# A tuned attention-and-MLP kernel: the opening by pairs of heads, FP32 dummies, a later v tail, six feature tiles begun early, w_out used by quarters

## The chip, the cores and the metric

The kernel runs on one core of a Trainium2 chip. The core has five engines that each work through their own list of instructions in order: TensorE (PE, matmuls; weight loads are shown as PEld), VectorE (DVE), ScalarE (ACT), GpSimd (POOL) and SyncE (SP). PE writes to PSUM only; DVE and ACT read it from there. SP and POOL issue the DMA transfers between HBM and SBUF. The metric is device time of one launch in microseconds, lower is better: 337.65 us as the median of 3 runs (337.59 to 338.38) for the kernel before.

## What is computed

Attention with a forget gate over 8 batches, 8 heads, 576 positions and a head size of 64, then an MLP with a tanh GELU over all 4608 tokens, model size 512, feature size 2048.

```python
scores = (1 / sqrt(D)) * q @ k.T
cum = cumsum(log(clip(f, 1e-4, 1.0)))            # along the positions
scores = where(causal, -1e9, scores + cum[:, None] - cum[None, :])
attn = softmax(scores)
x = (attn @ v).transpose(0, 2, 1, 3).reshape(B * S, H * D)
h = x @ w_in
g = 0.5 * h * (1 + tanh(c * (h + 0.044715 * h**3)))
out = g @ w_out
```

The decay splits into a factor for the query, which the softmax cancels, and a factor for the key. The kernel holds the latter in `wT` and multiplies v by it (`vw`); the same factors make the denominators.

## The kernel before

Four heads of a batch are a quad; there are 16, two for each batch. For a quad, q and k are loaded with a cast to bf16 (`load_qk`, POOL's queue) into one of two buffers and turned by DVE (`transpose_qk`). `score_round` computes transposed scores in three rounds r = 0, 1, 2 into two PSUM tiles of two banks, one for each pair of heads (`bank_pair`), and ACT takes the exp of each pair's tile into `pt`. Then come denominators (`denominators`, `reciprocals`) and two output products (`attn_out`, `normalise`) into `xT`. `make_vw` forms `vw` of a quad on POOL or DVE.

The MLP runs in chunks of 512 tokens. `mlp_in(j)` makes 16 feature tiles, two to a PSUM pair, with four matmuls each (dt = 0 to 3), and `gelu` writes `gT`. `mlp_out(j)` is a generator: each pull is one feature tile's matmul into an output tile of 128 tokens (16 pulls to a tile, 64 to a chunk), or four matmuls of 32 columns each where other tiled matmuls stand around it. The output tile lies in the PSUM pool "m", which has two buffers; after the sixteenth pull DVE copies it to `o_st` and SP stores it. `step(i, j, fill, fills)` weaves the three score rounds of quad i, the products of quad j and `fills[r]` pulls of the generator.

Everything is recorded under a manual schedule: an engine executes its instructions in the order in which the code records them.

What the change touches:

- `startup` (lines 379 to 455): the loads, the gate's cumulative sums, dummy matmuls on `blank` (`warm_up`), then quads 0 and 1 in "early" rounds without the last 64 queries (`early_rounds`), with the causal mask added on PE by a matmul of the identity with `lows` (line 200), `late_scores` for the last 64 queries, and the first chunk of the MLP. PSUM tags "s" (two pairs), "x" (one pair) and "p" (two banks) are shared out there. In before, four feature tiles are begun with dt = 0, 1 while DVE normalises quad 1.
- The loads on POOL's queue in the order of line 414 on: v of batch 0 (heads 4 to 7), four parts of w_in, q and k of quad 2, four quarters of w_out, q and k of quad 3, v of batch 1 (heads 0 to 3). Heads 0 to 3 of batch 0's v, and heads 4 to 7 of batch 1's, come over SP's queue.
- `mlp_out` (lines 347 to 366), and the pulls of batch 0 (lines 517 to 523): 6, then 10, 8, 8 in `step(2, ...)`, 4, 6, 5 in `step(3, ...)`, 6, 6, 5 in `step(4, ...)`.
- In `step`, `make_vw(2)` is recorded on DVE in round 2 (line 480), ahead of that round's pulls (line 481).

Of the kernel before, what the change touches and what calls it, by code (L numbers as in the profile page):

```python
# [8 lines left out]
FP32 = mybir.dt.float32  # L9
# [7 lines left out]
def kernel(  # L17
# [80 lines left out]
    blank = singles.tile([128, 512], BF16, name="blank")  # L98
# [18 lines left out]
    def load_v(b, eng=nc.sync, heads=slice(0, H)):  # L117
        return [eng.dma_start(
            out=v_nat[b % 2][r:, t, heads, :],
            in_=v[b, heads, s0:s0 + 128 - r, :].rearrange("h p d -> p h d"),  # L120
        ) for t, r, s0 in [(t, 0, 128 * t) for t in range(TAIL)] + [(TAIL, 128 - LAST, S - LAST)]]
# [48 lines left out]
    def scores(i, tiles, cols, k0, q0, nq, c0, m0=0, m=128, fresh=False):  # L170
        for c in cols:
            for h in range(4):
# [8 lines left out]
    def score_round(i, r, tags=("s", "s"), early=False):  # L181
        off, parts = (early_rounds if early else rounds)[r]
        n = sum(x[2] for x in parts)
        tiles = [bank_pair(x, "ps_s") for x in tags]
        if r == 0:
            for c in range(2):
                scores(i, tiles, (c,), 0, 0, 512, 0, 0, 64, True)
                scores(i, tiles, (c,), 64, 64, 448, 64, 64, 64, True)
                scores(i, tiles, (c,), S - LAST, S - LAST, LAST, 0, 64, 64)
        else:  # L190
            c0 = 0
            for (t, q0, nq) in parts:
                scores(i, tiles, range(2), 128 * t, q0, nq, c0, fresh=(c0 == 0))
                c0 += nq
        if early:
            for g in range(2):
                c0 = 0
                for (t, q0, nq) in parts:
                    for x in range(2):
                        nc.tensor.matmul(tiles[g][:, x, c0:c0 + 128], ident, lows[t > 0],  # L200
                                         start=False, stop=True, skip_group_check=True)
                    c0 += nq
        for g in range(2):
            nc.scalar.activation(pt[i % 2][:, 2 * g:2 * g + 2, off:off + n],  # L204
                                 tiles[g][:, :, 0:n], AF.Exp, scale=scale)
# [141 lines left out]
    def mlp_out(j):  # L347
# [5 lines left out]
        for n, c0, c1 in parts:  # L353
            ps = pools["m"].tile([128, D_MODEL], FP32, name="pso", tag="m")
            c = 128 * (n % 8)
            for ft in range(N_FT):
                w = out_cols[0]
                for m in range(0, 128, w):
                    nc.tensor.matmul(ps[m:m + w, c0:c1], gT[:, ft, c + m:c + m + w],  # L359
                                     w_out_sb[:, ft, c0:c1], start=(ft == 0),  # L360
                                     stop=(ft == N_FT - 1), skip_group_check=True)
                if ft == N_FT - 1:
                    st = ostage_pool.tile([128, D_MODEL], FP32, name="o_st", tag="o")
                    nc.vector.tensor_copy(st[:, c0:c1], ps[:, c0:c1])  # L364
                    nc.sync.dma_start(out=out[128 * n:128 * n + 128, c0:c1], in_=st[:, c0:c1])
                yield
# [12 lines left out]
    def startup():  # L379
# [8 lines left out]
        warm = pools["p"].tile([128, 512], FP32, name="warm", tag="p")  # L388
        warm_up(warm, 11)
# [17 lines left out]
        warm_up(warm, 6)  # L407
# [4 lines left out]
        after(load_v(0, heads=slice(0, 4))[0], q0)  # L412
        make_vw(0, nc.vector, 0, TAIL)
        after(load_v(0, nc.gpsimd, slice(4, 8))[0], k1)
# [18 lines left out]
        score_round(1, 1, ("x", "s"), True)  # L433
# [3 lines left out]
        make_vw(1, nc.vector, 0, TAIL)  # L437
        score_round(1, 2, ("s", "x"), True)
        late_scores()
        reciprocals(1, early_product(1, den_groups(1), single("po")))  # L440
        po = bank_pair("x", "po")
        nums = [early_product(1, out_groups(1, y), po[:, y, :]) for y in range(2)]
# [9 lines left out]
        for u in range(2):  # L452
            gelu(0, u, phs[u])
        for u in range(2, N_FT // 2):
            mlp_in(0, (u,), "x" if u % 3 == 2 else "s")
# [41 lines left out]
    with tc.manual_schedule():  # L497
# [6 lines left out]
        for b in range(B):  # L504
# [61 lines left out]
```

## Time and profile before

| | |
|---|---|
| median of 3 runs | 337.65 us (337.59 to 338.38) |
| the profiled execution | 338.67 us |
| its span, first to last instruction | 337.0 us |
| read from HBM, written | 36.85 MB, 9.44 MB |
| issues of v on POOL's queue (128 KB), median to landing | 8, 6.8 us |
| issues of w_in parts (512 KB), median to landing | 4, 11.0 us |
| issues of w_out quarters (512 KB), median to landing | 4, 17.8 us |

The profile is one execution on the chip. A row of the timeline gives the start in us from the first instruction, the length of a merged group of instructions, engine, source line, operation, tiles written and read, shape and count; in brackets stands the idle time of the engine before the group and what ended it. The chain of work that ended last is followed back from the end, at each step to what released an instruction. The table of stages gives the busy time of each engine in a stretch, the granted PE clock as a share, the busy share of the DMA engines and the bytes moved.

### The profile page before, as it was taken

To read this page: it belongs to the slowest core of one execution; us is meant where nothing else is said; L and a number is where in the kernel's file an instruction comes from. 1 tells how busy PE (TensorE), PEld (TensorE's weight loads), DVE (VectorE), ACT (ScalarE), POOL (GpSimd) and SP (SyncE) were. 2 spreads that over 40 slices of the span, in tenths; PEclk is the share of its full clock that TensorE was granted. 3 is DMA by queue.
4 is the path that set the end of the run, shared out by engine and by line. 5 is a ranking of instruction groups with operands and counts; after the bars stand their busy time and mean duration, and the time that the engine had idled before them with its cause. 6 is when DMAs were issued, how large, how long until landed. Compare 5 with 4: busy or idle time off the path is not lost.

```text
span 337.0 us, 10056 instructions
## 1 busy us (share of the span) xinstructions
PE 327.8 (97%) x4549; PEld 160.8 (48%) x4571; DVE 124.8 (37%) x174; ACT 191.3 (57%) x206; POOL 115.1 (34%) x159
## 2 busy tenths in 40 slices
PE   7979999999999999999999999999999999999996
PEld 2544534444444444444478444444444454444444
DVE  7682176622526144604442342524330450000121
ACT  4875777767565757467555756576647704553000
POOL 6833258924534145242725162405520300000000
PEclk9999999999999999999999999999999999999999
DMA  7999999696117801491029310921000110000112
GB/s 133 204 180 211 216 216 207 143 210 131 64 35 153 161 35 64 98 205 45 33 71 205 74 65 33 186 57 66 36 31 0 35 64 33 0 0 28 67 69 87
DMA packets 45578, 33.29 MB, mean 99 GB/s; under 512 B 34304, under 2 KB 34560, under 8 KB 45536
## 3 DMA queue, kind: packets, MB, share of 16 engines
q0 software_dynamic: 7232, 14.81, 24.3%
q1 hardware_dynamic: 38304, 17.85, 19.7%
q8 instruction: 35, 0.57, 0.7%
q14 instruction: 7, 0.06, 0.1%
HBM read 36.85 MB, written 9.44 MB: 137 GB/s over the span
## 4 chain that ended last, share of the span: by engine, by line
PE 93%; issue 2%; DVE 1%; ACT 1%; DMA 1%; POOL 0%; POOLq 0%
PE ps_h L323 37%; PE pso L359 36%; PE po L250 10%; PE ps_s L173 9%; ACT pt L204 1%; DMA f_sb<-in_f_dram 1%; PE ps_s L200 1%; PE warm L377 1%; DVE cum_sb L400 0%; POOL pt L229 0%; DVE kT L142 0%; DVE qT L142 0%; ACT f_sb L399 0%; POOLq L561 0%; DVE f_sb L398 0%
## 5 line engine op out<-in xcount | busy, mean ns | idle before, releaser
L359 PE MATMUL pso<-w_out_sb,gT 128*32 128x512 bf16 (+2 forms) x1669 | 133.4, 377 | 0.5 <-issue 0.3
L323 PE MATMUL ps_h<-xT,w_in_sb 128*128 128x512 bf16 (+1 forms) x625 | 125.9, 357 | 2.4 <-issue 1.7
L332 ACT ACTIVATE gT<-ps_h 128x1024 bf16<-128x1024 f32 (+1 forms) x81 | 74.1, 928 | 70.9 <-PE ps_h L323 70.9
L204 ACT ACTIVATE pt<-ps_s 128x1024 bf16<-128x1024 f32 (+1 forms) x96 | 91.1, 1002 | 40.9 <-PE ps_s L173 38.3
L323 PEld LDWEIGHTS <-w_in_sb 128*128 128x128 bf16 x640 | 61.9, 98 | 65.3 <-issue 5.2
L359 PEld LDWEIGHTS <-gT 128*32 128x32 bf16 (+1 forms) x1675 | 59.8, 97 | 55.0 <-issue 1.0
L229 POOL TENSOR_SCALAR_AFFINE_SELECT pt<-pt 128x512 bf16<-128x512 bf16 (+1 forms) x70 | 44.1, 638 | 101.0 <-ACT pt L204 99.9
L364 DVE COPY o_st<-pso 128x512 f32<-128x512 f32 (+1 forms) x37 | 24.9, 674 | 87.6 <-PE pso L359 87.6
L281 DVE STREAM_TRANSPOSE den<-po 128x576 f32<-128x576 f32 (+2 forms) x17 | 12.7, 748 | 70.0 <-PE po L250 70.0
L154 POOL TENSOR_TENSOR vw<-v_nat,wT 128x1280 bf16<-128x1280 f32 (+1 forms) x26 | 37.7, 1471 | 0.9 <-DVE rec L283 0.7
L291 DVE TENSOR_TENSOR xT<-po,rb 128x576 bf16<-128x576 f32 (+1 forms) x32 | 23.8, 748 | 34.9 <-PE po L250 34.8
L173 PE MATMUL ps_s<-qT,kT 32*128 32x64 bf16 (+8 forms) x944 | 33.4, 286 | 1.0 <-ACT pt L204 0.6
L250 PE MATMUL po<-pt,vw 128*32 128x64 bf16 (+6 forms) x768 | 27.5, 277 | 0.0
L173 PEld LDWEIGHTS <-kT 32*128 32x128 bf16 (+1 forms) x944 | 14.6, 97 | 24.3 <-issue 20.9
L142 DVE STREAM_TRANSPOSE kT<-k_c 128x576 f32<-128x576 f32 x16 | 19.9, 1245 | 10.0 <-DMA k_c<-in_k_dram 10.0
L142 DVE STREAM_TRANSPOSE qT<-q_c 128x576 f32<-128x576 f32 x16 | 19.9, 1242 | 1.4 <-DMA q_c<-in_q_dram 1.3
L250 PEld LDWEIGHTS <-vw 128*32 128x32 bf16 x832 | 13.6, 96 | 13.8 <-issue 7.1
L112 POOL DMA_DIRECT2D k_c<-in_k_dram x16 | 9.1, 570 | 30.0 <-DVE kT L142 24.7
L250 PE MATMUL po<-pt,w_bf 128*32 128x64 bf16 (+8 forms) x384 | 14.3, 276 | 0.1
L285 DVE STREAM_TRANSPOSE rb<-rec 128x576 f32<-128x576 f32 (+2 forms) x17 | 12.6, 743 | 0.6
L112 POOL DMA_DIRECT2D q_c<-in_q_dram x16 | 8.6, 535 | 8.5 <-DVE qT L142 5.7
L332 ACT ACT_TABLE_LOAD x8 | 10.3, 1283 | 0.1
(43 smaller groups left out, 72.4 us busy)
## 6 DMA issues: line engine op xcount, KB each, us to landing
out_dram<-o_st SPq DMA_DIRECT2D x35, 256.0 KB, 2.0
v_nat<-in_v_dram SPq DMA_DIRECT2D x24, 256.0 KB, 5.9
k_c<-in_k_dram POOLq DMA_DIRECT2D x16, 288.0 KB, 6.3
q_c<-in_q_dram POOLq DMA_DIRECT2D x16, 288.0 KB, 7.2
w_in_sb<-in_moe_w_in_dram POOLq DMA_DIRECT2D x4, 512.0 KB, 11.0
w_out_sb<-in_moe_w_out_dram POOLq DMA_DIRECT2D x4, 512.0 KB, 17.8
v_nat<-in_v_dram SPq DMA_DIRECT2D x14, 128.0 KB, 5.1
v_nat<-in_v_dram POOLq DMA_DIRECT2D x8, 128.0 KB, 6.8
```

What stands on the lines that cost most here:

```text
L112: return [nc.gpsimd.dma_start(out=dst[i % 2].rearrange("p a d -> p (a d)"), in_=src[b, h0:h0 + 4].rearrange("h (p a) d -> (h p) (a d)", p=32))
L142: nc.vector.transpose(out=dst[i % 2].rearrange("p s c -> p (s c)").bitcast(FP32) .rearrange("p (t a) -> p a t", a=S // 32), in_=src[i % 2] ...
L154: eng.tensor_mul(vw[i % 2][:p, slot:slot + z - a], v_nat[(i // QPB) % 2][:p, a:z, h0:h0 + 4, :], wT[:p, i, a:z, :].unsqueeze(3).to_broadca ...
L173: nc.tensor.matmul(tiles[h // 2][m0:m0 + m, h % 2, c0:c0 + nq], kT[i % 2][32 * h:32 * h + 32, k0:k0 + m, c], qT[i % 2][32 * h:32 * h + 32, ...
L204: nc.scalar.activation(pt[i % 2][:, 2 * g:2 * g + 2, off:off + n], tiles[g][:, :, 0:n], AF.Exp, scale=scale)
L229: nc.gpsimd.affine_select(out=p[p0:p1, :, o:o + 128], in_=p[p0:p1, :, o:o + 128], compare_op=ALU.is_ge, fill=0.0, base=0, pattern=[[0, 4]] ...
L250: nc.tensor.matmul(ps[r0:r0 + w.shape[-1], o:o + nq], w, rhs[:, h, col:col + nq], start=(n in fresh), stop=(n in (0, len(parts) - 1)), ski ...
L291: nc.vector.tensor_mul(xT[:, 2 * (i % QPB) + y, t0:t0 + n], po, rbs[i][:, 0:n])
L323: nc.tensor.matmul(ph[:, o:o + m], w[:, dt], xT[:, dt, a:a + m], start=(dt == 0 and o == 0), stop=(dt == N_DT - 1), skip_group_check=True)
L332: nc.scalar.activation(gT[:, 2 * u + y:2 * u + y + n, o:o + CHUNK], ph[:, y:y + n, :], AF.Gelu_apprx_tanh)
L359: nc.tensor.matmul(ps[m:m + w, c0:c1], gT[:, ft, c + m:c + m + w], w_out_sb[:, ft, c0:c1], start=(ft == 0), stop=(ft == N_FT - 1), skip_gr ...
L364: nc.vector.tensor_copy(st[:, c0:c1], ps[:, c0:c1])
```

## The change

Masks of the first round are added to PSUM ahead of its scores (`first_round`); all early rounds but the first are done for one pair of heads at a time (`early_pair`), with tags s, x in turn; dummies take FP32 operands of 256 columns and fall from 11, 6, 4, 4, 2 to 5, 3, 1; the tail of v of batch 0 is loaded by one transfer for all eight heads behind w_in; quarter 0 of w_out comes ahead of q and k of quad 2; `make_vw(1)` is split in two halves; six feature tiles instead of four are begun with dt = 0, 1; `mlp_out(0)` takes tiles 0 and 1 in turns of four features; and the pulls of batch 0 are shared out anew. Its core:

```diff
-    blank = singles.tile([128, 512], BF16, name="blank")
+    blank = singles.tile([128, 256], FP32, name="blank")
...
+    v_tiles = [(t, 0, 128 * t) for t in range(TAIL)] + [(TAIL, 128 - LAST, S - LAST)]
+
+    def load_v(b, eng=nc.sync, heads=slice(0, H), tiles=slice(0, NT)):
...
+    def add_lows(r, tile, fresh=False):
+        c0 = 0
+        for (t, q0, nq) in early_rounds[r][1]:
+            for x in range(2):
+                nc.tensor.matmul(tile[:, x, c0:c0 + 128], ident, lows[t > 0],
+                                 start=fresh, stop=True, skip_group_check=True)
+            c0 += nq
...
+    def early_pair(i, r, g, tag):
+        tiles = {g: bank_pair(tag, "ps_s")}
+        part_scores(i, r, tiles, (2 * g, 2 * g + 1), early_rounds)
+        add_lows(r, tiles[g])
+        exps(i, r, g, tiles[g], early_rounds)
+
+    def first_round():
+        tiles = [bank_pair("s", "ps_s") for _ in range(2)]
+        for g in range(2):
+            add_lows(0, tiles[g], True)
+        yield
+        part_scores(0, 0, tiles, range(4), early_rounds, True)
+        for g in range(2):
+            exps(0, 0, g, tiles[g], early_rounds)
+        yield
...
-        for n, c0, c1 in parts:
-            ps = pools["m"].tile([128, D_MODEL], FP32, name="pso", tag="m")
+
+        order = [(x, ft) for x in range(len(parts)) for ft in range(N_FT)]
+        if j == 0:
+            order[:2 * N_FT] = [(x, ft) for f0 in range(0, N_FT, N_FT // 4) for x in range(2)
+                                for ft in range(f0, f0 + N_FT // 4)]
+        pss = {}
+        for x, ft in order:
+            n, c0, c1 = parts[x]
+            if ft == 0:
+                pss[x] = pools["m"].tile([128, D_MODEL], FP32, name="pso", tag="m")
+            ps = pss[x]
...
-        warm_up(warm, 11)
+        warm_up(warm, 5)
...
-        warm_up(warm, 6)
+        first = first_round()
+        next(first)
+        warm_up(warm, 3)
...
         for c in range(2):
             for u in range(QPB):
                 load_w_in(c, u)
+        load_v(0, nc.gpsimd, tiles=slice(TAIL, NT))
+        load_w_out(0)
         load_qk(2)
-        for c in range(4):
+        for c in range(1, 4):
             load_w_out(c)
...
+        make_vw(1, nc.vector, 0, 2)
...
-        for r, tags, n in ((0, ("s", "s"), 4), (1, ("x", "s"), 4), (2, ("s", "x"), 2)):
-            score_round(0, r, tags, True)
-            warm_up(warm, n)
-        score_round(1, 0, ("s", "s"), True)
+        next(first)
+        early_pair(0, 1, 0, "x")
+        early_pair(0, 1, 1, "s")
+        early_pair(0, 2, 0, "s")
+        warm_up(warm, 1)
+        early_pair(0, 2, 1, "x")
+        early_pair(1, 0, 0, "s")
+        early_pair(1, 0, 1, "s")
+        early_pair(1, 1, 0, "x")
...
-        phs = [bank_pair("s", "ps_h") for _ in range(2)]
-        for dts in ((0, 1), (2,), (3,)):
-            for ft in range(4):
-                mlp_mm(0, ft, phs[ft // 2][:, ft % 2, :], dts)
-            if dts[0] == 0:
-                for y in range(2):
-                    normalise(1, y, nums[y])
+        phs = [bank_pair(tag, "ps_h") for tag in ("x", "s", "s")]
+        for ft in range(6):
+            mlp_mm(0, ft, phs[ft // 2][:, ft % 2, :], (0, 1))
+        for y in range(2):
+            normalise(1, y, nums[y])
+        for u in range(3):
+            for y in range(2):
+                mlp_mm(0, 2 * u + y, phs[u][:, y, :], (2, 3))
+            gelu(0, u, phs[u])
...
-                pull(fill, 6, 32)
+                pull(fill, 8, 32)
                 late_outputs(bank_pair("po", "po")[:, 0, :])
-                step(2, None, fill, (10, 8, 8))
-                step(3, 2, fill, (4, 6, 5))
-                step(4, 3, fill, (6, 6, 5))
+                step(2, None, fill, (8, 10, 10))
+                step(3, 2, fill, (4, 5, 5))
+                step(4, 3, fill, (5, 5, 4))
```

More of the change, by code (lines that the diff above doesn't have):

```diff
@@ L179, in scores, with exps, part_scores @@
                 )
-    def score_round(i, r, tags=("s", "s"), early=False):
-        off, parts = (early_rounds if early else rounds)[r]
+    def exps(i, r, g, tile, rounds=rounds):
+        off, parts = rounds[r]
         n = sum(x[2] for x in parts)
-        tiles = [bank_pair(x, "ps_s") for x in tags]
+        nc.scalar.activation(pt[i % 2][:, 2 * g:2 * g + 2, off:off + n], tile[:, :, 0:n], AF.Exp,
+                             scale=scale)
+    def part_scores(i, r, tiles, heads, rounds=rounds, ahead=False):
@@ L191, in score_round @@
             c0 = 0
-            for (t, q0, nq) in parts:
-                scores(i, tiles, range(2), 128 * t, q0, nq, c0, fresh=(c0 == 0))
+            for (t, q0, nq) in rounds[r][1]:
+                scores(i, tiles, range(2), 128 * t, q0, nq, c0, fresh=(c0 == 0), heads=heads)
                 c0 += nq
[L195 to L202, printed above, removed]
```

63 lines of the change are left out of this document (31 added, 32 removed).

## The prediction

> **What bounds the kernel now.** First the page's first and fourth part. TensorE (PE) is at work nearly throughout, and the chain that ended last runs over it, so a change counts by how much idle time it takes from PE or gives to it.
>
> ```profile
> span 337.0 us, 10056 instructions
> PE 327.8 (97%) x4549; PEld 160.8 (48%) x4571; DVE 124.8 (37%) x174; ACT 191.3 (57%) x206; POOL 115.1 (34%) x159
> PE 93%; issue 2%; DVE 1%; ACT 1%; DMA 1%; POOL 0%; POOLq 0%
> ```
>
> The change touches the opening and batch 0 alone, so I next read the chain of the first 45 us. What the change can reach in the opening are the masks (L200) on the chain, the dummies (L377) that the chain waits behind, and a hole of 1.54 us ahead of the third matmul round of the MLP, for which the profile names no cause.
>
> ```profile
> 9.04 0.33 PE ps_s L200 x4
> ...
> 9.42 0.81 PE warm L377 x3
> ...
> 11.55 0.86 PE warm L377 x4
> ...
> 13.17 0.43 PE warm L377 x2
> ...
> 23.50 1.54 issue
> 25.04 9.67 PE ps_h L323 x44
> ```
>
> Third, busy time by stage, for the DMA. The columns after the stretch are its length, the five engines' busy time, the granted clock, the busy share of the DMA engines and GB/s.
>
> ```profile
> 15.00:20.00 5.00, 4.50 (x156) 2.82 (x148) 3.96 (x6) 4.72 (x6) 3.27 (x6) 1.00 0.97 142
> 20.00:25.00 5.00, 3.44 (x82) 1.78 (x69) 4.11 (x9) 3.22 (x3) 1.41 (x2) 1.00 1.11 206
> ...
> 35.00:40.00 5.00, 5.00 (x164) 2.88 (x170) 0.87 (x4) 3.56 (x6) 1.52 (x3) 1.00 1.12 211
> 40.00:45.00 5.00, 4.84 (x57) 1.91 (x42) 2.53 (x4) 3.63 (x5) 1.95 (x5) 1.00 1.08 238
> 45.00:50.00 5.00, 4.83 (x84) 2.25 (x88) 3.61 (x5) 3.46 (x5) 2.50 (x4) 1.00 1.00 197
> ```
>
> The DMA engines are full until about 50 us, with loads alone. So what is loaded late lands when the sum of the bytes ahead of it has been moved, however early it was asked for, and a faster opening does not hasten it. The question for this change is therefore which of those landings PE meets when it comes earlier. Fourth, the timeline around 46 us:
>
> ```profile
> 46.24 1.67 PE L359 MATMUL pso<-w_out_sb,gT 128*128 128x512 bf16 x7 [0.16 <-issue]
> 46.46 1.82 DVE L154 TENSOR_TENSOR vw<-v_nat,wT 128x1280 bf16<-128x1280 f32 x2 [0.54 <-DMA v_nat<-in_v_dram]
> 47.84 0.91 PE L173 MATMUL ps_s<-qT,kT 32*64 32x512 bf16 x24
> 48.21 0.68 DVE L364 COPY o_st<-pso 128x512 f32<-128x512 f32 x1
> ```
>
> VectorE (DVE) waits 0.54 us for v of batch 1, heads 0 to 3, starts the multiplication of quad 2 (`make_vw(2)`) at 46.46, and only then copies out an output tile, at 48.21. Before, nobody minds: it is tile 1, and PE goes on into tile 2 at once, because tile 0 had been copied long ago and the pool "m" has two buffers.
>
> **The change part by part.** *Opening* (masks in front, pairs, dummies, the early half of `make_vw(1)`, six feature tiles). On ACT the exps of both quads stand nearly back to back, with a hole here and there, so pairs can save about the mask's 0.33 us and the holes' 0.47 and 0.29:
>
> ```profile
> 14.76 5.14 ACT L204 ACTIVATE pt<-ps_s 128x1024 bf16<-128x1024 f32 x6 [0.47 <-PE ps_s L200]
> 20.19 1.94 ACT L216 ACTIVATE pt_late<-ps_s 128x1024 bf16<-128x1024 f32 x2 [0.29 <-PE ps_s L173]
> ```
>
> That is 1.1 us; the dummies removed (0.81 + 0.86 + 0.43 = 2.10) stand beside these exps and give nothing of their own. Six tiles begin with 12 matmuls in place of 8 ahead of the late normalising, four more of 0.215 (below), 0.86 us of useful work into the hole of 1.54. Together 2.0 us; the bounds are 0 and 2.10 + 1.54 + 0.33 = 4.0. The FP32 dummies have no row. The nearest are the FP32 transposes of 64 columns beside the bf16 dummies:
>
> ```profile
> 1.26 4.31 PE L377 MATMUL warm<-blank 128*128 128x512 bf16 x11 [1.26 <-DVE blank L387]
> ...
> 6.21 0.49 PE L404 MATMUL small<-ident_f,cum_sb 64*128 64x64 f32 x5 [0.64 <-DVE cum_sb L400]
> 6.63 0.98 PEld L377 LDWEIGHTS <-blank 128*128 128x128 bf16 x6
> 6.63 1.47 PE L377 MATMUL warm<-blank 128*128 128x512 bf16 x6
> ```
>
> 0.49 / 5 is 0.1 us for 64 columns, so 0.4 for 256; at the slow pace of the first eleven (0.39 against 0.245 each) 0.6. Five then take 2.0 to 3.0 us and three 1.2, no more than the 4.31 and 1.47 they replace. I cost them at 0; were they twice as long, the scores would start about 2 us later, and the opening would lose its gain.
>
> *v tail behind w_in*: two transfers of 64 KB become one of 128 KB on the POOL queue. 128 KB at 206 GB/s is 0.6 us by which all four parts of w_in land sooner. It is used by `make_vw` of the tail, hidden under the features that follow. *w_out quarter 0 ahead of k and q of quad 2*: their order only; from w_out's second quarter on, the sequence of loads, with k and q of quad 3 and v of batch 1 behind it, has the same bytes ahead of it as before. So v of batch 1 still lands for a start of DVE at 46.46.
>
> *w_out by quarters*, and with it the step on which the time hangs. In `mlp_out(0)` tiles 0 and 1 now take turns, four features at a time, so tile 0 ends with the 28th matmul group and tile 1 with the 32nd, where tile 0 ended with the 16th. The fills of step 2 sum to 8 + 8 + 10 + 10 = 36 up to its end, where they were 6 + 10 + 8 + 8 = 32. So groups 33 to 36, the first of tile 2, stand on PE ahead of the scores of quad 3, and tile 2 needs the buffer of tile 0. Tile 0 can only be copied out in the last round of step 2, and there `step` records `make_vw(2)` on DVE ahead of the fills: both copies now queue on DVE behind a multiplication that waits for v. PE waits for the first copy; behind PE's wait stand the scores of quad 3 and all else on PE, and the exps of ACT.
>
> The sum. The copy ends at 48.21 + 0.68 = 48.89, the handover takes 0.04:
>
> ```profile
> 50.83 0.04 issue
> ```
>
> so PE goes on at 48.93. Before, PE had done the same work, 32 groups and the scores of step 2, by 47.84 at the latest. With the opening's 2.0 us it is there at 45.9 and stands idle for 3.0 us; with any gain from 0 to 4.0 it is there between 43.9 and 47.9, always ahead of 48.93. The opening's gain therefore falls out of the sum: the hold has to be paid from 47.84. The four groups come first, (1.67 - 0.38) / 6 = 0.215 each by the row of seven above (0.38 is the duration of one), 0.86 together; the scores of quad 3 start at 49.79, that is 1.95 later than before. They then find their buffers free, so the exps follow sooner:
>
> ```profile
> 39.79 0.66 PE L173 MATMUL ps_s<-qT,kT 32*64 32x512 bf16 x24
> ...
> 40.60 1.94 ACT L204 ACTIVATE pt<-ps_s 128x1024 bf16<-128x1024 f32 x2 [0.45 <-PE ps_s L173]
> ...
> 48.88 1.94 ACT L204 ACTIVATE pt<-ps_s 128x1024 bf16<-128x1024 f32 x2 [0.83 <-PE ps_s L173]
> ...
> 50.87 0.63 PE L173 MATMUL ps_s<-qT,kT 32*128 32x64 bf16 x14 [0.20 <-ACT pt L204]
> ...
> 51.58 1.94 ACT L204 ACTIVATE pt<-ps_s 128x1024 bf16<-128x1024 f32 x2 [0.76 <-PE ps_s L173]
> ...
> 54.26 1.94 ACT L204 ACTIVATE pt<-ps_s 128x1024 bf16<-128x1024 f32 x2 [0.74 <-PE ps_s L173]
> ...
> 57.62 1.47 PE L359 MATMUL pso<-w_out_sb,gT 128*32 128x512 bf16 x24
> ...
> 59.76 1.94 ACT L204 ACTIVATE pt<-ps_s 128x1024 bf16<-128x1024 f32 x2 [0.77 <-PE ps_s L173]
> ```
>
> 40.60 - 39.79 = 0.81 after the scores, so at 50.60 where it was 48.88: 1.72 late. Do the four groups done early come back in steps 3 and 4, whose fills fall from 32 to 28? A group there is 1.47 / 6 = 0.245 us, so 0.98 if PE sets the pace. But the exps follow each other at 2.70, 2.68 and so on up to 59.76, and the scores of a round wait for the exps of the one before (the 0.20 at 50.87): 0.74 from scores to exps and 1.94 of exps are 2.68. ACT and PE in turn set that pace, and shorter fills do not shorten it. Only the last round, which no exps follow, gets its one group back: 1.72 - 0.245 = 1.47, say 1.5. Behind it PE is dense, and I see nothing that would win it back.
>
> If PE sets the pace after all it is 1.95 - 0.98 = 0.97; if the fills give nothing back, 1.95. The profiled execution took 338.67, of which 337.0 are span and 1.7 lie around it; it would be 340.2. It stands 1.0 above the median of the runs, 337.65; from there it is **339.1**, 338.6 to 339.6 by these two bounds. What I can't price is the transfer of v: if the 128 KB of the tail now cost their 0.6 us twice, it lands that much later; if the stretch from 15 to 20 us, in which only 142 GB/s were moved, ran at 206, (206 - 142) x 5 / 206 = 1.6 us sooner. With these the range is 337.0 to 340.2.
>
> **The rivals.** *The DMA gains, and the hold shrinks to nothing:* v lands 1.6 us sooner, the copy ends at 47.3, and PE is about even: 339.1 - 1.6 = 337.5. For it speaks that the slow stretch is just where the order of loads changes; against it that the queue still issues as many transfers there.
>
> *The gain holds:* the opening's 2.0 us stay. That needs tile 0's copy by 45.9, v landed 3.0 us sooner: 337.65 - 2.0 = 335.7. The full DMA rows from 20 us on speak against it.
>
> *The clock drops in the idle time:* PE stands still for 3.0 us. [...] Against it: the granted clock is 1.00 in every row, the hole of 1.54 included; for it, that no hole of this size is in the trace. [...]
>
> *The change doesn't speed the opening:* two heads at a time fill half of the row groups, and PE could be late for the exps. Up to about 1 us of net loss it changes nothing, since the hold covers it (47.84 + 1.1 = 48.93); with 2 us lost 339.1 + 1.0 = 340.1.
>
> **How the numbers follow.** A measurement of this kernel tells about 0.3% from no change, 1.0 us. The forecast 0.58, of which some 0.06 end below 338.6 and so within it; the DMA gains 0.18; the gain holds 0.10; the clock 0.09; a slower opening 0.05. Faster: 0.10 and 0.02 of the DMA's case, 0.12. Same: 0.16 of the DMA's case and 0.06 of the forecast's, 0.22. Slower: the rest, 0.66. The range from 336.8 to 340.9 leaves out the gain that holds and the far end of the clock's case.
>
> **What would show it.** Right: a hole of about 3 us on PE ahead of the ninth group of the last round of step 2, ended by the copy of `o_st`, which ends near 48.9; the exps of quad 3 about 1.7 us later than 48.88; the hole of 1.54 us gone and the matmuls behind it, now from 25.04, about 2 us earlier. Wrong: the multiplication of quad 2 starting well before 46; or PE coming to that group after 48.9, so that the opening counts; or exps of quad 3 and 4 following each other in less than 2.6 us.

## The result, and the profile after

The changed kernel takes 341.72 us (median of four runs, 340.55 to 342.08) against 337.85 us (337.59 to 338.38) for the kernel before: 1.0107 times as long, with an interval from 1.0079 to 1.0134. It is slower, as forecast, but by 3.9 us where 339.1 meant some 1.5, and the time lies outside the range of 336.8 to 340.9. The profiled execution took 340.55 us, close to the 340.2 worked out for it.

The page of the changed kernel: PE has about 1 us more of work, and the span is 1.8 us longer than in the profiled execution before.

```profile
span 338.8 us, 10026 instructions
PE 328.9 (97%) x4535; PEld 163.6 (48%) x4556; DVE 125.3 (37%) x175; ACT 191.2 (56%) x206; POOL 115.6 (34%) x159
PE 82%; DMA 11%; issue 2%; POOL 2%; DVE 1%; ACT 1%; POOLq 0%; DVEq 0%
PE pso L394 33%; PE ps_h L350 33%; PE po L277 9%; PE ps_s L175 7%; DMA w_out_sb<-in_moe_w_out_dram 5%; DMA w_in_sb<-in_moe_w_in_dram 3%; DMA v_nat<-in_v_dram 2%; DMA k_c<-in_k_dram 2%; POOL v_nat L120 1%; DVE vw L156 1%; ACT pt L186 1%; POOL pt L256 0%; DVE o_st L399 0%; POOL w_in_sb L133 0%; POOLq L607 0%
```

In the chain of waits, DMA now has 11% instead of 1%. Before, the chain ran over PE right through the opening; now it leaves PE for the copy (`o_st`), the multiplication (`vw`), v, and behind v the loads of w_out and w_in.

The timeline of the changed kernel at that place (start, length, engine, line, operation, and in brackets the idle time and what ended it):

```profile
45.41 1.47 PE L394 MATMUL pso<-w_out_sb,gT 128*128 128x512 bf16 x5
46.26 2.26 DVE L156 TENSOR_TENSOR vw<-v_nat,wT 128x1280 bf16<-128x1280 f32 x2 [0.88 <-DMA v_nat<-in_v_dram]
48.44 1.27 DVE L399 COPY o_st<-pso 128x512 f32<-128x512 f32 x2
49.17 1.02 PE L394 MATMUL pso<-w_out_sb,gT 128*128 128x512 bf16 x4 [2.29 <-DVE o_st L399]
50.12 0.66 PE L175 MATMUL ps_s<-qT,kT 32*64 32x512 bf16 x24
50.93 1.94 ACT L186 ACTIVATE pt<-ps_s 128x1024 bf16<-128x1024 f32 x2 [3.41 <-PE ps_s L175]
```

PE ends group 32 at 46.88 and stands idle for 2.29 us. DVE has both copies to do, but `make_vw(2)` is ahead of them and waits for v until 46.26. The first of the two copies is tile 0's; with the 0.68 of a single copy it ends at 49.12, and PE goes on at 49.17. Then come the four groups, the scores of quad 3 at 50.12, and their exps at 50.93, 2.05 later than before.

The opening of the changed kernel:

```profile
1.26 4.63 PE L412 MATMUL warm<-blank 128*128 128x256 f32 x10 [1.26 <-DVE blank L422]
7.16 1.51 PE L412 MATMUL warm<-blank 128*128 128x256 f32 x6
9.36 7.58 ACT L186 ACTIVATE pt<-ps_s 128x1024 bf16<-128x1024 f32 x9 [1.53 <-PE ps_s L175]
17.31 1.02 ACT L186 ACTIVATE pt<-ps_s 128x1024 bf16<-128x1024 f32 x1 [0.37 <-PE ps_s L206]
19.07 1.15 ACT L186 ACTIVATE pt<-ps_s 128x512 bf16<-128x512 f32 x2 [0.73 <-PE ps_s L206]
22.75 13.76 PE L350 MATMUL ps_h<-xT,w_in_sb 128*128 128x512 bf16 x62 [0.16 <-issue]
```

The FP32 dummies (two records to each) take 4.63 us for five and 1.51 for three, nearly what they replace. The first exp comes at 9.36 (before 9.30): no gain there, and by pairs ACT now waits 0.37 and 0.73 us for masks. The features start at 22.75 instead of 21.81, but run without the hole of 1.54.

The rest of the 3.9 us is not in this execution. The other three of the four had spans of 340.1, 340.4 and 339.9 us at a mean granted clock of 0.994 to 0.995, where this one shows 0.999.

### The profile page after: what moved, and what is told of

The parts are those of the page before. It is cut to its first block, busy times and chain, and to the rows that moved or that the text cites. A ratio compares the mean times of both kernels' runs of the same rounds, so it can differ in the third digit from the quotient of the medians.

```text
span 338.8 us, 10026 instructions
## 1 busy us (share of the span) xinstructions
PE 328.9 (97%) x4535; PEld 163.6 (48%) x4556; DVE 125.3 (37%) x175; ACT 191.2 (56%) x206; POOL 115.6 (34%) x159
## 4 chain that ended last, share of the span: by engine, by line
PE 82%; DMA 11%; issue 2%; POOL 2%; DVE 1%; ACT 1%; POOLq 0%; DVEq 0%
PE pso L394 33%; PE ps_h L350 33%; PE po L277 9%; PE ps_s L175 7%; DMA w_out_sb<-in_moe_w_out_dram 5%; DMA w_in_sb<-in_moe_w_in_dram 3%; DMA v_nat<-in_v_dram 2%; DMA k_c<-in_k_dram 2%; POOL v_nat L120 1%; DVE vw L156 1%; ACT pt L186 1%; POOL pt L256 0%; DVE o_st L399 0%; POOL w_in_sb L133 0%; POOLq L607 0%
## 5 line engine op out<-in xcount | busy, mean ns | idle before, releaser
L175 PE MATMUL ps_s<-qT,kT 32*128 32x64 bf16 (+9 forms) x944 | 35.2, 285 | 1.0 <-ACT pt L186 1.0
L175 PEld LDWEIGHTS <-kT 32*128 32x128 bf16 (+1 forms) x944 | 15.3, 97 | 24.3 <-issue 19.2
```

The lines of the kernel that those rows point to most:

```text
L175: nc.tensor.matmul(tiles[h // 2][m0:m0 + m, h % 2, c0:c0 + nq], kT[i % 2][32 * h:32 * h + 32, k0:k0 + m, c], qT[i % 2][32 * h:32 * h + 32, ...
```

## The experiments

Every group of runs had the kernel before run beside it on the same chip. The theory was the hold: PE waits at group 33 for tile 0's copy, and everything behind follows the end of that copy. The rivals were the clock, and that the opening, not the hold, costs the time.

**The changed kernel again**, unaltered, to see how it varies.

> The changed kernel once more, for its clock. Of its four runs one had a granted clock of 0.999 and a span of 338.8 us, three had 0.994 to 0.995 and 339.9 to 340.4. Theory: in most executions the clock falls to half for some 3.4 us after PE has stood idle (2.29 us ahead of group 33). Then most runs show 0.994 to 0.995 again and spans 1.1 to 1.6 us above those at 0.999; a profile of such an execution shows the clock under 1 in a stretch that begins between 47 and 50 us. Rival: the clock falls in the opening, where fewer dummies run; then that stretch lies before 20 us. Second rival: the runs' clock has nothing to do with the kernel; then the kernel before shows 0.994 as often.

It took 340.6 us (339.34 to 342.88, six runs; 337.67 beside it): 1.0086 [1.0054, 1.0119]. The profiled execution happened to test the opening. Its second block of dummies took 2.88 us instead of 1.51, its first exp came at 11.13 instead of 9.36, and its timeline reads:

```profile
7.40 2.88 PE L412 MATMUL warm<-blank 128*128 128x256 f32 x6
...
46.27 2.26 DVE L156 TENSOR_TENSOR vw<-v_nat,wT 128x1280 bf16<-128x1280 f32 x2 [0.50 <-DMA v_nat<-in_v_dram]
...
48.46 1.27 DVE L399 COPY o_st<-pso 128x512 f32<-128x512 f32 x2
49.18 1.02 PE L394 MATMUL pso<-w_out_sb,gT 128*128 128x512 bf16 x4 [0.23 <-DVE o_st L399]
```

The second block runs at the pace of the first one (0.48 us a record against 4.63 / 10 = 0.46), where it took 0.25 in the first execution. PE comes 2 us later to group 33 and waits 0.23 us instead of 2.29, and it goes on at the same time, 49.18. The span is the same, 338.8 us. So 2 us of the opening are worth nothing here.

Two of the six executions, not most, show a clock of 0.994 or 0.995. The second rival falls: in all groups of runs together, the kernel before shows 0.998 or more in each of its 65 executions.

**The fills alone put back** on the changed kernel: group 33 no longer stands ahead of the scores of quad 3.

```diff
-                step(2, None, fill, (8, 10, 10))
-                step(3, 2, fill, (4, 5, 5))
-                step(4, 3, fill, (5, 5, 4))
+                step(2, None, fill, (8, 10, 6))
+                step(3, 2, fill, (4, 6, 5))
+                step(4, 3, fill, (6, 6, 5))
```

> The changed kernel with the fills (8, 10, 6), (4, 6, 5), (6, 6, 5): 32 groups before step 3, so that tile 2 is not begun ahead of the scores of quad 3. Theory (hold and clock): no idle time at group 33; the scores of quad 3 start at about 46.9 us, their exps some 0.5 us sooner than in the kernel before, the clock is 0.998 or more in every run, 337.0 to 337.6 us. Rival (the clock falls in the opening): 0.994 in most runs and about 338.8 us. Rival (steps 3 and 4 are paced by PE alone): all of the opening's 1.0 us is kept, 336.8 us.

It took 338.06 us (337.97 to 340.25, twelve runs), 1.0018 [1.0001, 1.0035]. The loss is all but gone, and so is any gain of the opening; 337.0 to 337.6 were expected. The clock is 0.998 or more in all twelve. Three of them take 339.86 to 340.25 us even so, which no profile here explains. Its timeline:

```profile
46.61 0.41 PE L175 MATMUL ps_s<-qT,kT 32*64 32x512 bf16 x2
47.36 0.66 PE L175 MATMUL ps_s<-qT,kT 32*64 32x512 bf16 x22 [0.34 <-ACT pt L186]
47.47 1.27 DVE L399 COPY o_st<-pso 128x512 f32<-128x512 f32 x2
48.15 1.94 ACT L186 ACTIVATE pt<-ps_s 128x1024 bf16<-128x1024 f32 x2 [0.84 <-PE ps_s L175]
```

The copies still stand late on DVE, to 48.74, but nobody waits for them. PE starts the scores at 46.61 and then waits for ACT, which is still at the exps of the round before. Against a usual execution of before (46.84 and 47.88, below) the scores begin 0.2 us sooner and the exps come 0.3 later, not 0.5 sooner.

**Work in the idle time**: nine dummy matmuls into PSUM that nothing reads, between groups 32 and 33 of the changed kernel. This leaves the hold and takes away PE's idle time.

```diff
-            pull(fill, fills[r], 128 if j is None else 32)
+            if (i, r) == (2, 2):
+                pull(fill, 6)
+                warm = bank_pair("po", "warm")[:, 0, :]
+                for _ in range(9):
+                    nc.tensor.matmul(warm, w_out_sb[:, 0, 0:128], w_out_sb[:, 0, :],
+                                     start=True, stop=True)
+                pull(fill, fills[r] - 6)
+            else:
+                pull(fill, fills[r], 128 if j is None else 32)
```

> The changed kernel with nine dummies of 512 columns ahead of group 33, which fill some 1.9 of the 2.29 us of idle time and go into a PSUM tile that nothing reads. Theory (the idle time drops the clock): the span of the profile stays near 338.8 us, every run has 0.998 or more, the median falls to about 340.5 us. Rival (the clock falls in the opening, or for another reason): 0.994 in most runs and 341.7 us as in the changed kernel.

```profile
46.53 2.11 PE L531 MATMUL warm<-w_out_sb 128*128 128x512 bf16 x9
47.67 1.27 DVE L399 COPY o_st<-pso 128x512 f32<-128x512 f32 x2
48.47 1.03 PE L394 MATMUL pso<-w_out_sb,gT 128*128 128x512 bf16 x4
```

Five of six executions took 339.81 to 340.81 us, 340.31 in the middle, at a clock of 0.999 or 1.00: 1.0071 [1.0055, 1.0087]. The sixth took 346.84 us at 0.980, against the expectation; it is not in the comparison, it has no profile, and nothing here explains it. In the profile PE is never idle at that place, and the five are still 2.6 us slower than the 337.67 beside them. So that much is the hold's own price, without any fall of the clock.

**The quarters and fills alone** on the kernel before; its opening and its loads stay.

```diff
+        order = [(x, ft) for x in range(len(parts)) for ft in range(N_FT)]
+        if j == 0:
+            order[:2 * N_FT] = [(x, ft) for f0 in range(0, N_FT, N_FT // 4) for x in range(2)
+                                for ft in range(f0, f0 + N_FT // 4)]
...
-                pull(fill, 6, 32)
+                pull(fill, 8, 32)
...
-                step(2, None, fill, (10, 8, 8))
+                step(2, None, fill, (8, 10, 10))
```

> The kernel before with one part of the change alone: tiles 0 and 1 by quarters and the new fills. Theory (hold): PE comes to group 33 at about 47.9 us and waits about 1.1 us for the copy behind the multiplication of quad 2, as late as in the changed kernel, so that the span is about 1.5 to 2.0 us over the kernel before (339.4 to 339.9 us); the idle time is only half as long, so the clock stays at 0.998 in most runs. Rival (the opening costs the time): no more than 0.5 us over the kernel before.

It took 339.7 us (339.45 to 339.92), 1.0052 [1.0038, 1.0067]. The hold stands here too, with less idle time since PE comes later, and the clock is 0.999 to 1.00 in all six:

```profile
46.12 1.82 DVE L154 TENSOR_TENSOR vw<-v_nat,wT 128x1280 bf16<-128x1280 f32 x2 [1.36 <-DMA v_nat<-in_v_dram]
...
47.86 1.27 DVE L371 COPY o_st<-pso 128x512 f32<-128x512 f32 x2
48.59 1.02 PE L366 MATMUL pso<-w_out_sb,gT 128*128 128x512 bf16 x4 [1.02 <-DVE o_st L371]
```

One part of the change, put alone on the kernel before, brings 2.0 us of loss.

**The kernel before, profiled again**, since the forecast had been worked out from a single execution that took 1.0 us longer than the median.

> The kernel before, for a second profile. Its runs have a median span of 336.0 us, the profile that the prediction read has 337.0. Theory: the end of the hold is set by the landing of v of batch 1, which no faster opening moves, so the lateness has to be counted from where a usual execution of the kernel before stands, not from the profiled one: a usual profile starts the scores of quad 3 about 1.0 us before 47.84, with v landing at much the same time (multiplication of quad 2 near 46.1 to 46.5). Rival: the scores of quad 3 start at 47.8 again, and the missing microsecond lies behind batch 0.

It took 337.96 us with a span of 336.0, where the fifteen runs of that kernel beside it have a median of 338.29 us. Over all groups, 65 other executions of it have spans from 335.6 to 337.5, with 336.2 in the middle; only six have 337.0, the span of the first profile, or more.

```profile
24.11 12.48 PE L323 MATMUL ps_h<-xT,w_in_sb 128*128 128x512 bf16 x57 [0.49 <-issue]
...
45.97 2.26 DVE L154 TENSOR_TENSOR vw<-v_nat,wT 128x1280 bf16<-128x1280 f32 x2 [0.95 <-DMA v_nat<-in_v_dram]
46.84 0.92 PE L173 MATMUL ps_s<-qT,kT 32*64 32x512 bf16 x24
...
47.88 1.94 ACT L204 ACTIVATE pt<-ps_s 128x1024 bf16<-128x1024 f32 x2 [0.84 <-PE ps_s L173]
```

The hole in the features is 0.49 us instead of 1.54, and the scores of quad 3 start at 46.84, 1.0 sooner than the 47.84 that the forecast counts from. The multiplication of quad 2 ends at 48.23 (45.97 + 2.26), as good as unmoved from 48.28. This is where the forecast's size went wrong (below).

**`make_vw(2)` behind the pulls** of its round, on the changed kernel, so that the copies no longer queue behind it.

```diff
-            if i is not None and r == {2: 2, 3: 1}.get(i, 0):
-                make_vw(i, nc.vector if i == 2 else nc.gpsimd)
+            if i is not None and i != 2 and r == {3: 1}.get(i, 0):
+                make_vw(i, nc.gpsimd)
             pull(fill, fills[r], 128 if j is None else 32)
+            if (i, r) == (2, 2):
+                make_vw(i, nc.vector)
```

> The changed kernel with the multiplication of quad 2 recorded on DVE behind the fills of that round, so behind both copies, and the fills left as they are. Theory (the hold is the queue on DVE): group 33 follows group 32 at about 46.7 us with no idle time, no clock under 0.998, the scores of quad 3 start near 47.5, 337.4 to 338.0 us. Rival (the buffer is late for another reason): the idle time stays.

```profile
45.80 2.41 PE L394 MATMUL pso<-w_out_sb,gT 128*128 128x512 bf16 x10
...
47.91 2.25 DVE L156 TENSOR_TENSOR vw<-v_nat,wT 128x1280 bf16<-128x1280 f32 x2
47.97 2.69 POOL L256 TENSOR_SCALAR_AFFINE_SELECT pt<-pt 128x512 bf16<-128x512 bf16 x2 [2.15 <-ACT pt L186]
48.14 0.66 PE L175 MATMUL ps_s<-qT,kT 32*64 32x512 bf16 x24
...
49.94 0.31 PE L277 MATMUL po<-pt,w_bf 128*1 128x320 bf16 x4 [0.56 <-POOL pt L256]
50.71 0.25 PE L277 MATMUL po<-pt,w_bf 128*1 128x192 bf16 x4 [0.46 <-POOL pt L256]
```

The hold goes: ten groups in one row, no idle time. But it took 339.0 us (1.003 [1.0015, 1.0046]), more than the 337.4 to 338.0 expected. The multiplication now runs at the same time as POOL's two masks of quad 2, which take 2.69 us in place of 1.26, and PE waits 0.56 and 0.46 us for them. A wait taken away on one engine came back through another.

**The changed kernel, two further executions**, in search of the clock.

> The changed kernel again, for a profile with a lowered clock (of ten executions five showed 0.994 or 0.995, the two profiled ones did not). Theory: half clock for about 3.4 us beginning between 47 and 53 us, that is after the idle time at group 33. Rival: it lies in the opening, before 20 us.

> As the run before it: the changed kernel, for a profile with a lowered clock, with the same two expectations.

They took 339.51 and 341.06 us, spans 337.8 and 339.3, both at a clock of 1.00; PE idles 1.30 and 1.77 us ahead of group 33. Neither shows the lowered clock, so its place in the changed kernel stays unseen, but they give two more points for the theory. In all seven profiled executions with the hold and a full clock (the one with BF16 dummies comes further on) the span is the end of tile 0's copy, 0.67 or 0.68 after its start, and 289.7 us:

| execution | `make_vw(2)` starts | copy ends | PE idle | span |
|---|---|---|---|---|
| changed, first | 46.26 | 49.12 | 2.29 | 338.8 |
| changed, again | 46.27 | 49.13 | 0.23 | 338.8 |
| changed, third | 45.65 | 48.07 | 1.30 | 337.8 |
| changed, fourth | 47.20 | 49.62 | 1.77 | 339.3 |
| dummies in the idle time | 45.92 | 48.34 | none | 338.1 |
| quarters and fills alone | 46.12 | 48.54 | 1.02 | 338.2 |
| BF16 dummies | 45.62 | 48.04 | 1.32 | 337.7 |

The copy's end varies by 1.6 us, PE's idle time by 2.3, and the span follows the copy alone.

**v of batch 1, heads 0 to 3, asked for later**, to lengthen the idle time.

```diff
-        load_v(1, nc.gpsimd, slice(0, 4))
...
             prepare(2)
+            load_v(1, nc.gpsimd, slice(0, 4))
```

> The changed kernel with the load of v of batch 1, heads 0 to 3, queued behind k and q of quad 4, which lengthens the idle time at group 33 on purpose. In six profiles with a hold (after, e1, e7, e8, e3, e4) the span is the end of tile 0's copy + 289.7 us, within 0.1. Theory (hold): v lands 2.5 to 3 us later, the copy ends at 51 to 52 us, PE stands idle for 4 to 5 us and the span is that end + 289.7, if the clock holds. Theory (idle time drops the clock by one window of 3.4 us): with so long a hole the clock falls in every run (0.994 to 0.995), the profile shows it between 47 and 56 us, and the span is 1 to 2 us more than the copy's end + 289.7. Rival (the clock falls in the opening): 0.998 or more in about half of the runs, as in the changed kernel.

It took 345.06 us (343.98 to 345.68, four runs), 1.0212 [1.0189, 1.0236], with a clock of 0.989 to 0.990 in all four. The timeline, and then the stages with busy time of PE, PEld, DVE, ACT and POOL, granted clock, DMA share and GB/s:

```profile
48.45 1.82 DVE L156 TENSOR_TENSOR vw<-v_nat,wT 128x1280 bf16<-128x1280 f32 x2 [4.64 <-DMA v_nat<-in_v_dram]
50.19 1.27 DVE L399 COPY o_st<-pso 128x512 f32<-128x512 f32 x2
...
50.92 1.86 PE L394 MATMUL pso<-w_out_sb,gT 128*128 128x512 bf16 x4 [4.29 <-DVE o_st L399]
```

```profile
45.00:47.00 2.00, 1.58 (x17) 0.60 (x7) 0.00 (x0) 1.68 (x2) 0.17 (x1) 1.00 1.11 213
47.00:50.00 3.00, 0.00 (x0) 0.00 (x0) 1.55 (x2) 0.26 (x1) 1.22 (x2) 0.81 0.85 149
50.00:53.00 3.00, 2.08 (x12) 0.60 (x19) 1.46 (x3) 0.00 (x0) 0.00 (x0) 0.50 0.42 144
53.00:56.00 3.00, 3.00 (x60) 1.32 (x48) 0.70 (x1) 1.94 (x2) 0.05 (x1) 0.55 1.06 226
56.00:60.00 4.00, 4.00 (x100) 1.80 (x96) 3.31 (x6) 2.22 (x3) 3.85 (x4) 1.00 0.91 156
```

PE is idle from 46.63 to 50.92. A mean of 0.81 over 47 to 50 is 1.00 for 1.86 us and 0.50 for the rest, so the clock falls at about 48.9, some 2.25 us after the idle time began; 0.55 over 53 to 56 puts its return at 55.7. The four groups take 1.86 us instead of 1.02. The copy ends at 50.87, and the span of 342.3 is that and 291.4: 1.7 more than in the table. That is the price of the clock: some 6.8 us at half, the first 2.0 of them in idle time.

**Six tiles and the order of loads, alone**, on the kernel before: v's tail behind w_in, w_out's quarter 0 in front, and six feature tiles begun. With the quarters out of it, the hole of 1.54 us was to go.

```diff
+        load_v(0, nc.gpsimd, tiles=slice(TAIL, NT))
+        load_w_out(0)
         load_qk(2)
...
-        po = bank_pair("x", "po")
-        nums = [early_product(1, out_groups(1, y), po[:, y, :]) for y in range(2)]
-        phs = [bank_pair("s", "ps_h") for _ in range(2)]
...
+        nums = [early_product(1, out_groups(1, y), single("po")) for y in range(2)]
+        phs = [bank_pair(tag, "ps_h") for tag in ("x", "s", "s")]
+        for ft in range(6):
+            mlp_mm(0, ft, phs[ft // 2][:, ft % 2, :], (0, 1))
...
```

> The kernel before with its opening rounds, dummies, fills and order of tiles, and with two parts of the change: the order of loads (v tail behind w_in, first quarter of w_out ahead of quad 2) and six feature tiles begun. Theory: the hole ahead of the third matmul round (0.49 us in a usual execution, 1.54 in the one first profiled) goes, some 0.45 us come on top through the two banks of products on tag p, as in the changed kernel, and steps 3 and 4 keep their pace: 0 to 0.5 us faster than the kernel before, 337.3 to 338.0 us. Rival (the six tiles are worth their four matmuls): 0.9 us faster.

It took 338.5 us (337.56 to 340.38, twelve runs), 1.0017 [0.9999, 1.0034]: nothing won. In the profiled execution the hole is still there, behind the same first feature matmuls, though PE comes to it at 25.08 instead of 23.50:

```profile
26.51 2.77 PE L325 MATMUL ps_h<-xT,w_in_sb 128*128 128x512 bf16 x12 [1.43 <-issue]
```

**BF16 dummies** in the changed kernel, to see whether the FP32 operands have a part in the clock.

```diff
-    blank = singles.tile([128, 256], FP32, name="blank")
+    blank = singles.tile([128, 512], BF16, name="blank")
...
-        warm_up(warm, 5)
+        warm_up(warm, 11)
...
-        warm_up(warm, 3)
+        warm_up(warm, 5)
...
-            warm_up(warm, 1)
+            warm_up(warm, 2)
```

> The changed kernel with bf16 dummies of 512 columns (11, 5 and 2) in place of the FP32 ones. Theory (hold): the opening does not count, so the span is the end of tile 0's copy + 289.7 us again, and the clock is 0.994 to 0.995 in some runs as in the changed kernel: median 339.5 to 341.8 us. Rival (the FP32 dummies cost the time or the clock): all runs at 0.998 or more and at least 1 us less than the changed kernel's median.

It took 339.87 us (339.44 to 342.03, six runs), 1.0074 [1.0045, 1.0103]. Two of the six have a clock of 0.995, with spans of 340.3 and 339.9; the other four have 0.999 or 1.00 and 337.7 to 338.2. So the clock does not come from the FP32 dummies.

**The kernel before without the ten dummies of its early rounds**, to shift PE's list of instructions and see whether the hole shifts with it.

```diff
-        for r, tags, n in ((0, ("s", "s"), 4), (1, ("x", "s"), 4), (2, ("s", "x"), 2)):
+        for r, tags, n in ((0, ("s", "s"), 0), (1, ("x", "s"), 0), (2, ("s", "x"), 0)):
```

> The kernel before without the ten dummies between its opening rounds. In it and in e5, e4 and e10 PE stood idle for 0.3 to 1.5 us with no releaser, each time behind the 703rd to 705th record of PE and PEld, at the 8th feature matmul in three of them and at the 8th of a different order in e10, whatever the loads. Theory (a block of instructions has not been fetched): with 20 instructions fewer in front, the same place in the stream is the 18th feature matmul, which runs at about 25.5 us, when the block has come; no such hole, feature matmuls without a gap, 0.3 to 0.8 us faster than the kernel before. Rival (the hole belongs to the change from dt = 0, 1 to dt = 2, or to the load of w_in): it stays at the 8th or 9th feature matmul.

The hole goes: the 23 feature matmuls from 21.75 on run as one. But the time is the same, 338.04 us against 338.14 (0.9993 [0.998, 1.0006]), not 0.3 to 0.8 less. PE then meets the last quarter of w_out:

```profile
21.75 5.59 PE L323 MATMUL ps_h<-xT,w_in_sb 128*128 128x512 bf16 x23
...
40.82 1.02 PE L359 MATMUL pso<-w_out_sb,gT 128*128 128x512 bf16 x4 [0.52 <-DMA w_out_sb<-in_moe_w_out_dram]
```

No version beat the kernel before by more than the noise. Where the hold or the hole is taken out, the next wait stands close behind: ACT's exps (0.34), POOL's masks (0.56 and 0.46), w_out's last quarter (0.52).

## Why the prediction was wrong

*The hold: right.* PE stood ahead of group 33, released by `o_st`, as the forecast had it. The copy's end was given as 48.89 and is 49.12; PE goes on at 49.17 (forecast 48.93), the scores start at 50.12 (49.79), the exps at 50.93 (50.60). DVE got v 0.20 us sooner than in the profile before, but its multiplication took 2.26 instead of 1.82. The idle time is 2.29 and not 3.0, since the opening brought PE there 1.0 us earlier instead of 2.0.

*"The opening's gain therefore falls out of the sum": right*, shown by the execution with 2 us less of it and the same span. The gain itself was mis-sized. Exps by pairs won nothing (they wait 0.37 and 0.73 us for masks), and against a usual execution of before, in which the hole is 0.49, PE comes to this place hardly earlier: there the scores of quad 3 start at 46.84, here group 32 ends at 46.88, and with the fills put back the scores start at 46.61. FP32 dummies at 0: right but for the execution in which three took 2.88 us, though five took 4.63 us where 2.0 to 3.0 had been worked out.

*What is given back: right.* The forecast takes 1.95 of late scores to 1.47 at the end, 0.48. Before, the span is the start of those scores and 289.2 (47.84 and 337.0, 46.84 and 336.0); after, 50.12 and 288.7. The difference is 0.5.

***"It stands 1.0 above the median of the runs, 337.65; from there it is 339.1": this step failed.*** It takes the +1.47, worked out against an execution that was 1.0 us late, and adds it to a usual one. But the hold is no fixed delay; its end is set by v's landing and the multiplication behind it, and does not move with PE's arrival. A usual execution reaches the scores at 46.84 instead of 47.84 and then waits for the same copy. The prediction had written that the hold "has to be paid from 47.84"; a usual execution pays it from 46.84. So the 1.0 had to stay in: 50.12 - 46.84 = 3.28 of late scores, less 0.48, is 2.8, and 336.0 + 2.8 is the measured 338.8. In the prediction's own terms, 340.2 was the forecast for any execution, and no 1.0 was to be taken off. The copy's end, 0.2 later than forecast, is the rest. The runs without a fall of the clock agree: seven of them have spans from 337.6 to 339.3, 338.8 in the middle, which with the 1.7 around it is 340.5 us.

*The rival of the clock, given 0.09, came beside the forecast.* Of the twelve executions of the changed kernel five show a clock of 0.994 or 0.995, three of them among the first four. Against the 0.999 of the others that is 0.005 x 340 / 0.5 = 3.4 us at a clock of 0.50, the one that the profile with the later v shows; this is an estimate. Their spans average 340.3 against 338.5 for the others, so it costs 1.8 us each time, and it lifts the median of the first four from about 340.5 to 341.72 (two of the next six have it, and their median is 340.6). The range up to 340.9 counts in a price for this case that no run shows; what the runs showed are these 1.8 us. Of the 3.9 us, then, 2.7 are the hold, where the forecast had 1.5, and 1.2 the clock. With the changed opening and no idle time at group 33, the clock falls in none of 22 executions (first row of the table), so the opening is not where it falls. It goes with the idle time:

| kernel | PE idle at group 33 where profiled | executions at 0.995 or less |
|---|---|---|
| fills put back; `make_vw(2)` later | none | 0 of 12; 0 of 10 |
| dummies in the idle time | none | 0 of the 5 compared (the sixth: 0.980) |
| quarters and fills alone | 1.02 | 0 of 6 |
| BF16 dummies | 1.32 | 2 of 6 |
| changed kernel | 0.23 to 2.29 | 5 of 12 |
| v later | 4.29 | 4 of 4 |

The four profiles of the changed kernel are all without the fall. That it falls at group 33 there is argued from this table, the profile with the later v and the windows below, and was not seen in the kernel itself.

*The other rivals:* v landed 0.2 us sooner, not 1.6, so the gains of the DMA did not come. The gain did not hold even with the hold taken out (338.06). A slower opening was covered by the hold, as the prediction said.

## What to carry to other kernels

Where a step waits for a landing, its end does not move with the arrival of the engine that waits (here PE went on at 49.17 and at 49.18, having waited 2.29 and 0.23 us): reckon each execution's loss from its own arrival, and never carry a difference from a late execution over to the median. Before more work is pulled ahead of a critical product, see which buffer it needs, which engine frees it, and what that engine has in front of it. An idle hole of PE can cost more than its length: in these profiles every window of 3.41 us with 1.38 us or less of PE work was followed by one at a granted clock of 0.50.

## What the runs showed that was not expected

**The clock fell 2.25 us after PE's last matmul.** With v later it was down at 48.88, and stayed at 0.50 for 6.83 us, twice 3.41; the 44.37 us at full clock before it are 13 times that, and the 331.09 in the kernel before are 97 times. From these lengths the clock is read here as set anew every 3.41 us, in windows. The window that ended at 48.88 had begun at 45.46 and had 1.12 us of PE work, about a third, so it was not wholly idle.

How much work is too little can be read from all fourteen profiles, cut into windows of 3.41 us from where their clock changes. In each of them the clock also falls at the end, where PE runs out of work (at 335.96 in the kernel before). Every window with at most 1.38 us of PE work is followed by a clock of 0.50, every one with 1.57 or more by 1.00. The cases nearest to the border (times in us):

| execution | window | PE busy in it | clock after it |
|---|---|---|---|
| kernel before | 332.55 to 335.96 | 1.19 | 0.50 |
| v later | 45.46 to 48.88 | 1.12 | 0.50 |
| v later | 48.88 to 52.29 | 1.37 | 0.50 |
| without round dummies | 331.62 to 335.04 | 1.38 | 0.50 |
| `make_vw(2)` later | 332.84 to 336.26 | 1.57 | 1.00 |
| changed, fourth | 47.01 to 50.43 | 1.65 | 1.00 |
| changed, first | 47.76 to 51.17 | 2.00 | 1.00 |

By these rows 1.8 to 2.0 us of idle time were enough, where one window held them (3.41 - 1.57 and 3.41 - 1.38). In the changed kernel's first execution a border, at 47.76, divides the 2.29 us; in the fourth, 1.77 us are just too few. With the border elsewhere, or a later v, the same rows would give a fall, which fits five of twelve. The two that fell with BF16 dummies have spans some 2 us longer than the others; how long PE stood idle in them was not seen.

In the kernel without round dummies six of twelve executions show 0.989 to 0.995 too, and their spans are only some 0.5 us longer (336.3 to 337.2 against 336.0 to 336.4); where it falls there was not profiled.

**A mask on POOL and a multiplication on DVE were slower together (1.39 us for 0.64, 2.26 for 1.82).** `make_vw(2)` is two instructions. Grouped by form, with the mean ns behind the busy time, the kernel before, in whose profile the masks come only at 48.11, when the second instruction has begun:

```profile
L229 POOL TENSOR_SCALAR_AFFINE_SELECT pt<-pt 128x512 bf16<-128x512 bf16 x3 | 1.9, 641 | 1.9 <-ACT pt L204 1.8
L154 DVE TENSOR_TENSOR vw<-v_nat,wT 128x1280 bf16<-128x1280 f32 x1 | 1.5, 1493 | 0.5 <-DMA v_nat<-in_v_dram 0.5
L154 DVE TENSOR_TENSOR vw<-v_nat,wT 64x256 bf16<-64x256 f32 x1 | 0.4, 408 | 0.0
```

and the timeline of the changed kernel when it ran again, where a mask starts during the first instruction:

```profile
46.87 1.39 POOL L256 TENSOR_SCALAR_AFFINE_SELECT pt<-pt 128x512 bf16<-128x512 bf16 x1 [1.34 <-ACT pt L186]
```

and, in its groups by form, the second instruction:

```profile
L156 DVE TENSOR_TENSOR vw<-v_nat,wT 64x256 bf16<-64x256 f32 x1 | 0.8, 850 | 0.0
```

The mask takes 1.39 us instead of 0.64, and ends 0.50 after that first instruction (46.27 + 1.49 = 47.76); the second then takes 850 ns instead of 408. In the six executions where the two take 2.25 or 2.26 together, a mask was still running when the second began, and it ended 0.49 us after the first, to 0.01; where they take 1.82, none was running when the second began (once a mask began with it, to 0.01 us, and then the mask took 0.91). The times are those of a mask that waits for the first instruction, and a second instruction that waits for the mask; why they would wait, no run shows. The delay is 0.44 us of the hold in the first two executions of the changed kernel, and lies behind PE's waits of 0.56 and 0.46 us in the version with `make_vw(2)` later.

**The hole without a cause goes with the count of PE's instructions, and ends behind a packet on a queue of instructions.** In the executions with it, it comes behind the same number of matmuls and weight loads to within two (the counts of the first two columns of busy time), early or late. The stages up to the hole, before, before again, and six tiles alone:

```profile
0.00:23.40 23.40, 20.61 (x349) 10.37 (x351) 17.75 (x31) 17.05 (x20) 15.23 (x31) 1.00 0.94 169
```

```profile
0.00:23.50 23.50, 20.87 (x351) 10.41 (x351) 17.55 (x31) 17.01 (x20) 16.23 (x32) 1.00 0.96 171
```

```profile
0.00:25.00 25.00, 21.02 (x349) 10.43 (x351) 18.46 (x31) 17.07 (x20) 15.60 (x32) 1.00 0.96 175
```

With ten matmuls and their weight loads fewer in front, and the same work after them, it goes, but for 0.06 us at 25.65, behind 701 of them. The traces also list the packets of the DMA queues. On a queue of the kind "instruction" one packet of 16 KB lands shortly before PE goes on, each time (in us):

| execution | matmuls and weight loads before | packet landed | PE goes on | idle time |
|---|---|---|---|---|
| kernel before | 700 | 23.52 | 25.04 | 1.54 |
| before, again | 702 | 22.73 | 24.11 | 0.49 |
| quarters and fills alone | 700 | 22.69 | 24.11 | 0.27 |
| six tiles alone | 700 | 25.14 | 26.51 | 1.43 |
| without round dummies | 701 | 24.08 | 25.65 | 0.06 |

PE goes on 1.4 to 1.6 us after the landing in all five, though the landing moves by 2.4 us. The changed kernel comes to that count at 25.77, 1.7 us after its packet (24.08), and has no hole. So the hole looks like a wait for PE's next instructions, which would come through DMA engines that are full then (a share of 1.11 from 20 to 25 us). That is argued from these times; nothing here shows whose instructions the packet holds.
